# One unit less to spare, loads sized by the lead, a merged cache layout and the inverse root on GpSimd in a two-layer decode kernel

## Chip, cores, metric

One core of a Trainium2 chip. The metric is the device time of one launch in microseconds, as the median of several executions. The kernel before takes 2435.75 us (2431.96 to 2438.01, 12 runs).

## The reference

Two identical layers of attention over a cache, each followed by a small MLP, for one new token in each of 8 sequences. The same caches serve both layers, and the second layer's queries depend on the first layer's result.

```python
B, Sq, D = 8, 1, 640;  Hq, Hkv, Sk, Dh = 32, 32, 4096, 128;  Dff = 1728      # bf16
q = (layernorm(x) @ wq) per head;  p = softmax(q k^T / sqrt(Dh));  o = p v   # k, v: B x 32 x 4096 x 128
x = x + (o @ wo);   x = x + relu(layernorm(x) @ w1) @ w2
# ... and both lines once more, with the same k, v and weights
```

One cache is 8 x 32 x 4096 x 128 x 2 bytes = 268 MB. K and V, read in both layers, are 1074 MB. That is what the kernel is about.

## The kernel before

The work is cut into *visits*: a layer, a sequence `b` and a pair of heads `hp` (16 pairs). A visit reads a K tile and a V tile of 2 MB each. A tile has four *units* of 0.5 MB (128 partitions x 4 KB). SBUF holds an arena of 26 units. A planner in Python writes one static list of loads and engine work. Some units, loaded for layer 0, are kept until layer 1 of the same sequence, so they are not loaded twice. Between the two layers of `b`, the first four head pairs of sequence `b+1` have to pass through whatever units are left (`SPARE`), which take turns: a small ring; meanwhile the MLP of `b` and the queries of its layer 1 are worked off in small steps between the units.

```python
UNIT = 4; GP = 4; G = 26; SPARE = 6; SMALL = 4; AHEAD = 4; CAP = 20
...
    keep = set()                                   # the last pairs of heads; order1 visits them first
    for hp in order1:                              # order1 = 15, 14, 13, 0, 1, ...
        for which in "VK":
            for g in range(UNIT - 1, -1, -1):
                if len(keep) < G - SPARE:
                    keep.add((which, hp, g))
...
    def feed():                                    # called after every release of a unit
            ...
            roomy = G - len(kept)
            n = 4 if keeping or roomy >= 16 else 2 if roomy >= SMALL else 1
            while n > 1 and (g % n or any(...)):   # aligned, within the tile, same keeping
                n //= 2
            u = room(n)                            # n free units in a row, aligned to n
            if u is None:
                return
...
    def do_load(which, i, g, n, u):                # 16 KiB from one partition's row to the next
        src = (A_k_cache if which == "K" else A_v_cache)[b, hp]
        nc.sync.dma_start(out=arena[:, u * GW : (u + n) * GW], in_=src[:, g * GW : (g + n) * GW])
...
    def inverse_root(out, s2):                     # 1/sqrt for a layer norm of one sequence, all on VectorE
        ...                                        # four small instructions
        for n in range(4):                         # Newton steps
            nc.vector.scalar_tensor_tensor(out=v[:, 1:2], in0=y, scalar=v[:, 0:1], in1=y, op0=ALU.mult, op1=ALU.mult)
            nc.vector.scalar_tensor_tensor(out=dst, in0=v[:, 1:2], scalar=1.5, in1=y, op0=ALU.add, op1=ALU.mult)
```

## Time and profile before

| what | before | where it is read |
|---|---|---|
| time, median | 2435.75 us | 12 runs |
| bytes on the load queue | 1004.9 MB | DMA queues of the page |
| rate over the span / undisturbed / in a dip | 415 / 429 to 430 / about 361 GB/s | page, stretches |
| DMA in the chain that ended last | 82% | chain of waits |
| last load landed, span ended | 2416.1, 2432.6 us | completion counts in the trace |

The lines below are from the page of the kernel before: the DMA rows of the span in 40 equal slices (busy tenths, then GB/s), the load queue (packets, megabytes, share of 16 engines' span), the chain that ended last, and the issues by source (count, KB each, median us from issue to landing).

```profile
DMA  9999999999999999999999999999999999999997
GB/s 408 429 430 383 429 429 430 428 373 430 430 429 429 374 428 430 430 427 370 429 430 429 417 389 429 430 429 404 396 429 430 430 394 404 430 429 417 395 429 298
...
q1 hardware_dynamic: 83332, 1004.90, 98.6%
...
DMA 82%; PE 15%; DVE 2%; issue 1%; ACT 1%; SPq 0%; ACTq 0%
...
arena<-in_A_v_cache_dram SPq DMA_DIRECT2D x192, 2048.0 KB, 26.9
arena<-in_A_k_cache_dram SPq DMA_DIRECT2D x184, 2048.0 KB, 27.3
arena<-in_A_k_cache_dram SPq DMA_DIRECT2D x112, 1024.0 KB, 9.7
arena<-in_A_v_cache_dram SPq DMA_DIRECT2D x80, 1024.0 KB, 7.4
```

The engines are "busy" throughout, but the GB/s row shows the dips: one per sequence, eight in all. Two views say what is different in a dip. First, two stretches, an undisturbed one and most of a dip (busy time of each engine, clock, DMA share, GB/s); then what PE waited for in that dip (us in total, times, longest).

```profile
core 0: us, PE busy (x) PEld busy (x) DVE busy (x) ACT busy (x) POOL busy (x), PEclk, DMA share, GB/s
300.00:480.00 180.00, 81.81 (x1665) 47.79 (x1664) 23.14 (x117) 21.99 (x72) 0.00 (x0) 1.00 1.01 429
500.00:550.00 50.00, 39.14 (x854) 27.72 (x847) 13.30 (x75) 9.71 (x42) 0.00 (x0) 1.00 0.96 361
...
PE o_ps L458 <- DMA arena<-in_A_v_cache_dram: 10.3, 5, 4.8
PE s_ps L470 <- DMA arena<-in_A_k_cache_dram: 2.2, 4, 1.0
PE blk_ps L489 <- DVE diag L486: 1.8, 1, 1.8
```

In the undisturbed stretch PE works 82 of 180 us and only follows the loads. In the dip it still waits for loads, while the load queue waits for units to come free: the DMA share stays at 0.96, yet the rate falls to 361. The packets show it: those of the 1 MB loads took 334 ns on average at a median of 309, and a packet that is held up counts as busy. The rate is what to read. The third wait is VectorE's: a small reduction of the softmax stood behind the inverse root. The timeline of VectorE and PE (start, duration, line, instruction) shows it:

```profile
506.92 0.16 DVE L348 TENSOR_SCALAR root<-ch_ps 128x1 f32<-128x1 f32 x1 [0.61 <-PE ch_ps L330]
...
509.15 0.16 DVE L358 SCALAR_TENSOR_TENSOR rstd<-root 128x1 f32<-128x1 f32 x1
509.35 0.17 DVE L340 TENSOR_TENSOR xf<-xc,rstd 128x5 bf16<-128x5 f32 x1
509.43 0.27 DVE L484 TENSOR_REDUCE hmx<-blk_ps 2x1 f32<-2x128 f32 x1
509.73 0.15 DVE L486 TENSOR_TENSOR diag<-ident,hmx 2x2 bf16<-2x2 bf16 x1
509.94 0.16 PE L489 MATMUL blk_ps<-diag,onesb_c 2*128 2x2 bf16 x1 [1.82 <-DVE diag L486]
```

### The profile page before, as it was taken

The numbers are of one execution on the slowest core, as the hardware profiler recorded it, in microseconds if no ns is written. First come the engines' busy times: TensorE is split into PE (matmuls) and PEld (weight loads), VectorE is DVE, ScalarE is ACT, GpSimd is POOL, SyncE is SP. The second block draws the span as 40 slices with busy tenths as digits, with TensorE's granted clock in tenths as the row PEclk, the third lists the DMA queues.
The fourth block names the chain that finished last, engine by engine and source line by source line (L and its number), as shares of the span: only waits on it lengthen the run. The fifth ranks groups of instructions, "written<-read, shape, count | busy, mean of one in ns | idle before, by whom it ended". The sixth has DMA issues, their size and how long they took to land.

```text
span 2432.6 us, 57320 instructions
## 1 busy us (share of the span) xinstructions
PE 1272.9 (52%) x26486; PEld 788.4 (32%) x26486; DVE 380.7 (16%) x1984; ACT 337.4 (14%) x1179; POOL 0.7 (0%) x6
## 2 busy tenths in 40 slices
PE   3436644465444754447444574445744457445745
PEld 2224322343222422225222352223422234223523
DVE  1102111121111211112111121111211112111211
ACT  1101111111111111111111111111111111111111
POOL 0000000000000000000000000000000000000000
DMA  9999999999999999999999999999999999999997
GB/s 408 429 430 383 429 429 430 428 373 430 430 429 429 374 428 430 430 427 370 429 430 429 417 389 429 430 429 404 396 429 430 430 394 404 430 429 417 395 429 298
DMA packets 83572, 1008.57 MB, mean 415 GB/s; under 512 B 9348, under 2 KB 9348, under 8 KB 9348
## 3 DMA queue, kind: packets, MB, share of 16 engines
q1 hardware_dynamic: 83332, 1004.90, 98.6%
q8 instruction: 207, 3.39, 0.5%
q14 instruction: 33, 0.27, 0.0%
HBM read 1004.86 MB, written 0.01 MB: 413 GB/s over the span
## 4 chain that ended last, share of the span: by engine, by line
DMA 82%; PE 15%; DVE 2%; issue 1%; ACT 1%; SPq 0%; ACTq 0%
DMA arena<-in_A_k_cache_dram 42%; DMA arena<-in_A_v_cache_dram 38%; PE s_ps L470 5%; PE o_ps L458 5%; DMA w_sb<-in_B_w_dram 2%; PE q_ps L442 1%; DVE hmx L484 1%; DMA wo_sb<-in_A_wo_dram 1%; ACT o_sb L516 1%; PE oy_ps L521 1%; PE blk_ps L489 0%; DVE diag L486 0%; PE oy_ps L538 0%; PE blk_ps L480 0%; PE ch_ps L374 0%
## 5 line engine op out<-in xcount | busy, mean ns | idle before, releaser
L458 PE MATMUL o_ps<-arena,P_sb 128*4 128x512 bf16 x4096 | 556.9, 606 | 579.2 <-DMA arena<-in_A_v_cache_dram 575.8
L470 PE MATMUL s_ps<-q,arena 128*128 128x1 bf16 x16384 | 534.8, 165 | 510.4 <-DMA arena<-in_A_k_cache_dram 505.2
L470 PEld LDWEIGHTS <-arena 128*128 128x128 bf16 x16384 | 495.4, 104 | 539.1 <-DMA arena<-in_A_k_cache_dram 532.5
L458 PEld LDWEIGHTS <-P_sb 128*4 128x4 bf16 x4096 | 105.0, 83 | 681.8 <-issue 673.6
L493 ACT ACTIVATE nmax<-blk_ps 128x2 f32<-128x2 f32 x256 | 44.0, 172 | 1803.8 <-PE blk_ps L489 1803.8
L484 DVE TENSOR_REDUCE hmx<-blk_ps 2x1 f32<-2x128 f32 x256 | 71.3, 279 | 686.9 <-PE blk_ps L480 686.9
L516 ACT CAST o_sb<-o_ps 100x512 bf16<-100x512 f32 x256 | 149.8, 585 | 105.8 <-PE o_ps L458 105.8
L508 DVE TENSOR_REDUCE lsum<-blk_ps 128x2 f32<-128x64 f32 x256 | 57.5, 225 | 402.3 <-PE blk_ps L502 402.3
L497 ACT ACTIVATE P_sb<-s_ps,nmax 128x32 bf16<-128x32 f32 x512 | 119.0, 283 | 8.2
L476 DVE TENSOR_REDUCE mrow<-s_ps 128x2 bf16<-128x64 f32 x256 | 57.4, 224 | 252.9 <-PE s_ps L470 252.9
L502 PEld LDWEIGHTS <-onesb_c 128*128 128x128 bf16 x256 | 26.5, 104 | 203.6 <-issue 203.6
L480 PE MATMUL blk_ps<-ident,mrow 128*2 128x128 bf16 x256 | 79.5, 310 | 3.4 <-DVE mrow L476 3.4
L489 PEld LDWEIGHTS <-onesb_c 2*128 2x128 bf16 x256 | 25.2, 99 | 135.9 <-issue 135.9
L521 PE MATMUL oy_ps<-gsel,o_sb 100*128 100x2 bf16 x1024 | 63.8, 166 | 3.9 <-ACT o_sb L516 0.7
L531 DVE TENSOR_TENSOR oT<-oy_ps,invL 128x2 bf16<-128x2 f32 x128 | 20.4, 159 | 281.1 <-PE oy_ps L521 281.1
L531 DVE TENSOR_TENSOR o<-oy_ps,invL 128x2 bf16<-128x2 f32 x128 | 21.4, 167 | 274.7 <-PE oy_ps L521 274.7
L489 PE MATMUL blk_ps<-diag,onesb_c 2*128 2x2 bf16 x256 | 41.1, 160 | 42.7 <-DVE diag L486 14.4
L502 PE MATMUL blk_ps<-P_sb,onesb_c 128*128 128x64 bf16 x256 | 59.9, 234 | 1.1 <-ACT P_sb L497 1.1
L442 PE MATMUL q_ps<-xq,wq_sb 128*128 128x1 bf16 x1280 | 53.7, 166 | 4.2 <-issue 2.6
L538 PE MATMUL oy_ps<-oT,wo_sb 128*128 128x1 bf16 x1280 | 51.8, 165 | 0.0
L538 PEld LDWEIGHTS <-wo_sb 128*128 128x128 bf16 x1440 | 50.9, 105 | 0.8 <-issue 0.8
L442 PEld LDWEIGHTS <-wq_sb 128*128 128x128 bf16 x1280 | 44.9, 105 | 17.5 <-issue 16.7
(58 smaller groups left out, 408.3 us busy)
## 6 DMA issues: line engine op xcount, KB each, us to landing
arena<-in_A_v_cache_dram SPq DMA_DIRECT2D x192, 2048.0 KB, 26.9
arena<-in_A_k_cache_dram SPq DMA_DIRECT2D x184, 2048.0 KB, 27.3
arena<-in_A_k_cache_dram SPq DMA_DIRECT2D x112, 1024.0 KB, 9.7
arena<-in_A_v_cache_dram SPq DMA_DIRECT2D x80, 1024.0 KB, 7.4
wq_sb<-in_A_wq_dram SPq DMA_DIRECT2D x4, 1280.0 KB, 25.2
wo_sb<-in_A_wo_dram SPq DMA_DIRECT2D x4, 1280.0 KB, 35.8
w_sb<-in_B_w_dram SPq DMA_DIRECT2D x1, 2240.0 KB, 37.4
w_sb<-in_B_w_dram SPq DMA_DIRECT2D x1, 2160.0 KB
```

What stands on the lines that cost most here:

```text
L442: nc.tensor.matmul(q_ps[:, h : h + 1], lhsT=wq_sb[:, g, c, (2 * n + h) * Dh : (2 * n + h + 1) * Dh], rhs=xlns[b][:, 0, c : c + 1], start=( ...
L458: nc.tensor.matmul(o_ps[32 * c : 32 * c + CJ, :], lhsT=P_tiles[i][:, h, j : j + CJ], rhs=arena[:, at + c * CJ * Dh : at + (c + 1) * CJ * D ...
L470: nc.tensor.matmul(s_tiles[i][:, j : j + 1], lhsT=arena[:, at + n * P : at + (n + 1) * P], rhs=q, start=True, stop=True)
L480: nc.tensor.matmul(blk[i][:2, :P], lhsT=m_tiles.pop(i), rhs=ident, start=True, stop=True)
L484: nc.vector.tensor_reduce(out=hmx, in_=blk[i][:2, :P], axis=AX.X, op=ALU.max)
L489: nc.tensor.matmul(blk[i][:, P : P + 2], lhsT=ones_b, rhs=nmax.pop(i), start=True, stop=True)
L497: nc.scalar.activation(out=P_tiles[i][:, h, :], in_=S[:, h, :], func=ACT.Exp, bias=nm[:, h : h + 1], scale=inv_sqrt_dh)
L502: nc.tensor.matmul(blk[i][:, P + 2 :], lhsT=ones_p, rhs=P_tiles[i].rearrange("p h j -> p (h j)"), start=True, stop=True)
L508: nc.vector.tensor_reduce(out=L, in_=blk.pop(i)[:, P + 2 :].rearrange("p (h j) -> p h j", h=2), axis=AX.X, op=ALU.add)
L516: nc.scalar.copy(out=o_tiles[i][:OR], in_=o_ps[:OR, :].rearrange("p (j d) -> p j d", j=CJ))
L521: nc.tensor.matmul(oy[i][:, :2], lhsT=o_tiles[i][:OR, j, :], rhs=gsel[:OR, j, :], start=(j == 0), stop=(j == CJ - 1))
L538: nc.tensor.matmul(oy[i][:, 2 + c * nb : 2 + (c + 1) * nb], lhsT=wo_sb[:, 2 * hp + h, c * P : (c + 1) * P], rhs=o1[:, 2 * hp + h, :] if la ...
```

## The change

Its intent is to read fewer bytes and to keep the loads flowing. (1) One more unit is kept (`SPARE = 5`). (2) The size of a load follows the *lead*, the number of occupied units that are not kept: up to 8 units with a large lead, single units when the lead is small; kept units follow the same rule, where before they always came four at a time. (3) K and V go into one array in the order in which they are used, so that a load can run over tiles. (4) The last loads taper. (5) The inverse root moves to GpSimd, with three Newton steps instead of four and one more empty step before its result is used.

```diff
-SPARE = 6
-SMALL = 4
+SPARE = 5
+LEADS = ((12, 8), (8, 4), (7, 2))
+PASSING = ((16, 8), (13, 4), (11, 2))
+def tile_at(NP, which, hp):
+    return max(0, 2 * hp - 1) if which == "K" else min(2 * hp + 2, 2 * NP - 1)
...
     def room(n):
-        us = [u for u in range(0, G - n + 1, n) if not any(owner[u : u + n])]
+        us = [u for u in range(G - n + 1) if not any(owner[u : u + n])]
...
-            roomy = G - len(kept)
-            n = 4 if keeping or roomy >= 16 else 2 if roomy >= SMALL else 1
+            lead = sum(owner) - len(kept)
+            leads = PASSING if kept else LEADS
+            most = next((n for least, n in leads if lead >= least), 1)
+            most = min(most, max(1, (len(stream) - at[0]) // 2))
+            b, p, keeping = place(stream[at[0]])
+            n = 1
+            while n < most and place(stream[at[0] + n]) == (b, p + n, keeping):
+                n += 1
...
-        norm = [(0, "sums"), (2, "mean"), (0, "center"), (2, "var"), (0, "scale"), (1, None)]
+        norm = [(0, "sums"), (2, "mean"), (0, "center"), (2, "var"), (0, "scale"), (1, None), (1, None)]
...
-        nc.sync.dma_start(out=arena[:, u * GW : (u + n) * GW], in_=src[:, g * GW : (g + n) * GW])
+        nc.sync.dma_start(out=arena[:, u * GW : (u + n) * GW], in_=A_kv[b, :, p * GW : (p + n) * GW])
...
-        for n in range(4):
-            nc.vector.scalar_tensor_tensor(...)          # two per step, on VectorE
+        for n in range(3):
+            nc.gpsimd.tensor_tensor(out=t, in0=y, in1=y, op=ALU.mult)
+            nc.gpsimd.tensor_scalar(out=t, in0=t, scalar1=v[:, 0:1], scalar2=1.5, op0=ALU.mult, op1=ALU.add)
+            nc.gpsimd.tensor_tensor(out=dst, in0=t, in1=y, op=ALU.mult)
...
+    kv = np.empty((B, p, 2 * NP, 2 * Sk), A_k_cache.dtype)   # a partition's 32 tiles: 512 KiB
```

A side effect: neighbouring partitions' rows were 16 KiB apart in HBM, and a tile was one contiguous piece; now they are 512 KiB apart.

More of the change, by code (lines that the diff above doesn't have):

```diff
@@ L60, in plan @@
         layer, b, hp = visits[i]
-        gs = [g for g in range(UNIT) if layer == 0 or (which, hp, g) not in keep]
-        stream.append((which, i, gs))
+        stream += [(which, i, g) for g in range(UNIT) if layer == 0 or (which, hp, g) not in keep]
     weights = {}
@@ L70, in plan @@
     weights.setdefault(max(1, NP - 4), []).append(("w2",))
-    owner = [None] * G
+    owner = [False] * G
     freed = list(range(-G, 0))
@@ L75, in plan, with place @@
     ops, chains = [], []
-    at = [0, 0, 0]
+    at = [0, 0]
     def keeps(which, i, g):
         return visits[i][0] == 0 and (which, visits[i][2], g) in keep
+    def place(x):
+        return visits[x[1]][1], tile_at(NP, x[0], visits[x[1]][2]) * UNIT + x[2], keeps(*x)
     def room(n):
-        us = [u for u in range(0, G - n + 1, n) if not any(owner[u : u + n])]
+        us = [u for u in range(G - n + 1) if not any(owner[u : u + n])]
         return min(us, key=lambda u: max(freed[u : u + n])) if us else None
@@ L88, in feed @@
         while at[0] < len(stream):
-            which, i, gs = stream[at[0]]
-            if at[1] == len(gs):
-                at[:2] = at[0] + 1, 0
-                continue
-            if at[1] == 0 and which == "K":
-                ops.extend(("weights",) + w for w in weights.pop(i, []))
-            g = gs[at[1]]
-            keeping = keeps(which, i, g)
-            roomy = G - len(kept)
-            n = 4 if keeping or roomy >= 16 else 2 if roomy >= SMALL else 1
-            while n > 1 and (g % n or any(x not in gs or keeps(which, i, x) != keeping for x in range(g, g + n))):
-                n //= 2
+            lead = sum(owner) - len(kept)
[6 more added lines that the diff above has]
+                n += 1
             u = room(n)
@@ L103, in feed @@
                 return
-            for k in range(n):
+            for k, (which, i, g) in enumerate(stream[at[0] : at[0] + n]):
+                ops.extend(("weights",) + w for w in weights.pop(i, []) if which == "K")
                 owner[u + k] = True
-                where[which, i, g + k] = u + k
+                where[which, i, g] = u + k
                 if keeping:
-                    kept[which, visits[i][1], visits[i][2], g + k] = u + k
-            ops.append(("load", which, i, g, n, u))
-            at[1] += n
+                    kept[which, b, visits[i][2], g] = u + k
+            ops.append(("load", b, p, n, u))
+            at[0] += n
     def find(which, i, g):
@@ L122, in release @@
             u = kept.pop(key)
-        at[2] += 1
-        owner[u], freed[u] = None, at[2]
+        at[1] += 1
+        owner[u], freed[u] = False, at[1]
         feed()
@@ L210 @@
     A_x: bass.AP,
-    A_k_cache: bass.AP,
-    A_v_cache: bass.AP,
+    A_kv: bass.AP,
     A_wq: bass.AP,
@@ L224 @@
     B, Sq, D = A_x.shape
-    _, NP, Dh, W = A_k_cache.shape
-    H = 2 * NP
+    H = A_wo.shape[1] // D
+    NP = H // 2
+    Dh = A_kv.shape[1]
+    W = A_kv.shape[2] // (2 * NP)
     Sk = W // 2
@@ L335, in scale @@
                 inverse_root(rstd, st[key, "var"])
+                nc.gpsimd.tensor_scalar(
+                    out=xln[:, 0, :], in0=st[key, "xc"][:, 0, :], scalar1=rstd, scalar2=None, op0=ALU.mult
+                )
             else:
@@ L339, in scale @@
                 nc.vector.reciprocal(out=rstd, in_=std)
-            nc.vector.tensor_tensor(out=xln, in0=st[key, "xc"], in1=_free(rstd, [(1, nb), (0, DC)]), op=ALU.mult)
+                nc.vector.tensor_tensor(out=xln, in0=st[key, "xc"], in1=_free(rstd, [(1, nb), (0, DC)]), op=ALU.mult)
         return dict(sums=sums, mean=mean, center=center, var=var, scale=scale)
@@ L348, in inverse_root @@
         nc.vector.tensor_scalar(out=v[:, 0:1], in0=s2, scalar1=1.0 / D, scalar2=eps, op0=ALU.mult, op1=ALU.add)
-        nc.vector.tensor_scalar(out=i[:, 1:2], in0=i[:, 0:1], scalar1=1, scalar2=None, op0=ALU.logical_shift_right)
-        nc.vector.tensor_scalar(
-            out=i[:, 2:3], in0=i[:, 1:2], scalar1=-1.0, scalar2=1597463007.0, op0=ALU.mult, op1=ALU.add
+        nc.gpsimd.tensor_scalar(
+            out=i[:, 2:3], in0=i[:, 0:1], scalar1=-0.5, scalar2=1597463007.0, op0=ALU.mult, op1=ALU.add
         )
-        nc.vector.tensor_scalar(out=v[:, 0:1], in0=v[:, 0:1], scalar1=-0.5, scalar2=None, op0=ALU.mult)
+        nc.gpsimd.tensor_scalar(out=v[:, 0:1], in0=v[:, 0:1], scalar1=-0.5, scalar2=None, op0=ALU.mult)
         y = v[:, 2:3]
-        for n in range(4):
-            nc.vector.scalar_tensor_tensor(out=v[:, 1:2], in0=y, scalar=v[:, 0:1], in1=y, op0=ALU.mult, op1=ALU.mult)
-            dst = out if n == 3 else v[:, 3:4] if n % 2 == 0 else v[:, 2:3]
-            nc.vector.scalar_tensor_tensor(out=dst, in0=v[:, 1:2], scalar=1.5, in1=y, op0=ALU.add, op1=ALU.mult)
+        t = v[:, 1:2]
+        for n in range(3):
+            nc.gpsimd.tensor_tensor(out=t, in0=y, in1=y, op=ALU.mult)
+            nc.gpsimd.tensor_scalar(out=t, in0=t, scalar1=v[:, 0:1], scalar2=1.5, op0=ALU.mult, op1=ALU.add)
+            dst = out if n == 2 else v[:, 3:4] if n == 0 else v[:, 2:3]
+            nc.gpsimd.tensor_tensor(out=dst, in0=t, in1=y, op=ALU.mult)
             y = dst
@@ L419, in do_finish, with do_load @@
             steps[2] = steps[2] or op == "add"
-    def do_load(which, i, g, n, u):
-        layer, b, hp = visits[i]
-        src = (A_k_cache if which == "K" else A_v_cache)[b, hp]
-        nc.sync.dma_start(out=arena[:, u * GW : (u + n) * GW], in_=src[:, g * GW : (g + n) * GW])
+    def do_load(b, p, n, u):
+        nc.sync.dma_start(out=arena[:, u * GW : (u + n) * GW], in_=A_kv[b, :, p * GW : (p + n) * GW])
     def do_q0(g):
@@ L550 @@
                 L=do_l, I=do_i, OC=do_oc, OG=do_og, O=do_o, W=do_w, Y=do_y, C=do_finish, Q0=do_q0, Q=do_q, QC=take_q)
-    with tc.manual_schedule(engines={ENG.PE, ENG.DVE, ENG.Activation, ENG.SP}):
+    with tc.manual_schedule(engines={ENG.PE, ENG.DVE, ENG.Activation, ENG.Pool, ENG.SP}):
         xT_ps = ps.tile([P, B * DC], FP32, name="ch_ps")
@@ L577, in _laid_out @@
     w2[:Dff] = B_w2
+    k = A_k_cache.reshape(B, NP, 2, Sk, Dh).transpose(0, 1, 4, 2, 3).reshape(B, NP, Dh, 2 * Sk)
+    v = A_v_cache.reshape(B, NP, 2, UNIT, NJ // UNIT, p, Dh).transpose(0, 1, 5, 3, 2, 4, 6).reshape(B, NP, p, -1)
+    kv = np.empty((B, p, 2 * NP, 2 * Sk), A_k_cache.dtype)
+    for hp in range(NP):
+        kv[:, :, tile_at(NP, "K", hp)] = k[:, hp]
+        kv[:, :, tile_at(NP, "V", hp)] = v[:, hp]
+    kv = kv.reshape(B, p, -1)
     return {
         "A_x": c(A_x),
-        "A_k_cache": c(A_k_cache.reshape(B, NP, 2, Sk, Dh).transpose(0, 1, 4, 2, 3)).reshape(B, NP, Dh, 2 * Sk),
-        "A_v_cache": c(A_v_cache.reshape(B, NP, 2, UNIT, NJ // UNIT, p, Dh).transpose(0, 1, 5, 3, 2, 4, 6)).reshape(
-            B, NP, p, 2 * NJ * Dh
-        ),
+        "A_kv": kv,
         "A_wq": c(A_wq.reshape(DC, p, NG, HD // NG).transpose(1, 2, 0, 3)).reshape(p, -1),
```

## The prediction

> **What bounds it.** Part 2 of the page has the DMA engines at 9 tenths or more in every slice but the last, mean 415 GB/s; the chain of waits is 82% DMA. PE is busy 52%. Part 3 counts 1004.9 MB on the load queue. In undisturbed stretches the stretch table shows 429 to 431 GB/s with 2 MB loads. At that rate the bytes need about 2337 us of the 2433. The other 95 us are about 14 us at the ends (the last load lands at about 2416) and eight dips, one per batch, of about 50 us each at about 355 GB/s (slices of 370 to 390), some 8 us lost in each. A dip is where 20 units of 0.5 MB are kept for the second layer and the next batch's first four head pairs pass through 6 spare units as 1 MB loads. There PE waits for arena loads (10.3 us for V alone in 500 to 545 us), and the queue for PE: latency of a small ring.
>
> **What the change does, on the critical path.**
> 1. SPARE 5 keeps one more unit per batch: 8 x 0.524 MB = 4.2 MB fewer, about -10 us.
> 2. Passing with 5 single units instead of 3 pairs. The shortest time from issue to landing is 5.2 us for a pair, so about 2.7 us fixed plus 2.5 transfer. A pair's cycle is 5.2 + about 2.1 on PE + 0.2 = 7.5 us against 7.4 us of transfer for three: no slack. A single's is about 2.7 + 1.2 + 1.0 + 0.2 = 5.1 us against 6.1: one us of slack. An issue costs the queue only 0.33 us. The ceiling falls: 8 KB rows take 309 ns, 16 KB rows 611 ns, so about 6 ns per row, and 4 KB rows would reach about 416 GB/s. I expect about 395 in the dips: -30 us over eight dips (at best -50), and +6 us for more single loads around them.
> 3. Loads of up to 8 units (32 KB rows) outside the dips: 430 to 432 GB/s, about -8 us.
> 4. Tapered last loads: one unit instead of four for PE after the last landing, -2 us.
> 5. Inverse root on GpSimd: frees some 2.6 us of DVE twice a batch; an added empty step covers its latency. Near zero outside item 2.
>
> The sum is -44 us: 2392.
>
> **The cost I can't size.** The merged layout makes consecutive partitions' rows 512 KiB apart in HBM (before: 16 KiB, whole tiles contiguous). The Trainium skill, "DMA: Bandwidth & Descriptors", section "Latency and other measured facts", has copies at a 512 KiB row pitch at 207 GB/s against 214 in full, 3% less. No trace here shows it. That would be +70 us; I give it less than even odds and add a few us.
>
> **Prediction: 2398 us, 2366 to 2450 in 8 of 10.** Chances: faster by over 2% 0.32, within 2% 0.62, slower by over 2% 0.06.
>
> **What would show it.** Load bytes 1000.7 MB. Steady stretches at 430 to 432 GB/s: item 3 right and no pitch loss; at 415 to 425: pitch loss, with 16 engines still fully busy and packets slower per byte. Dips at 385 to 410 instead of 355: item 2 right. PE's waits for xf near zero: item 5 right. Last landing to end a few us shorter: item 4.
>
> **What would make it wrong.** A pitch loss of over 2%; GpSimd stalling PE before the up-projection; single loads draining the buffer; or dips staying at 355.

## The result

| | before | after |
|---|---|---|
| time, median | 2435.75 us | 2391.67 us (2389.81 to 2395.99, 8 runs) |
| ratio | | 0.9822 (95%: 0.9812 to 0.9831) |
| bytes on the load queue | 1004.9 MB | 1000.7 MB |
| mean of the page's slices at 425 GB/s or more | 429.3 | 431.2 GB/s |
| dips: microseconds lost against 430 GB/s, eight together | 62.6 | 36.2 us |
| last load landed to end of span | 16.5 | 14.4 us |

Ratios here are the mean time of one kernel's fast runs over that of the other's of the same rounds, so not quite the ratio of the medians quoted. The row on dips is worked out from the trace's DMA packets: the rate in each microsecond, and 1 - rate/430 summed over the stretches around the eight passings where the rate, smoothed over 8 us, is below 424. It is one profiled execution per kernel, so a few us of it are chance.

The page of the kernel after, the lines that answer to those of before:

```profile
DMA  9999999999999999999999999999999999999997
GB/s 410 431 429 405 429 431 433 426 402 432 429 434 423 394 433 429 433 423 401 432 432 431 416 411 434 430 432 406 413 430 431 432 407 424 430 432 415 411 433 308
...
q1 hardware_dynamic: 99028, 1000.72, 99.3%
...
DMA 78%; PE 17%; DVE 1%; issue 1%; ACT 1%; POOL 1%; SPq 0%; ACTq 0%; DVEq 0%
...
arena<-in_A_kv_dram SPq DMA_DIRECT2D x129, 4096.0 KB, 24.7
arena<-in_A_kv_dram SPq DMA_DIRECT2D x423, 512.0 KB, 6.5
arena<-in_A_kv_dram SPq DMA_DIRECT2D x78, 2048.0 KB, 22.4
```

The dips of the GB/s row went from between 370 and 396 (lowest slice of each) to between 394 and 411, and the slices between them from 429 to 431. The same dip as before, and PE's waits in it. By the definition above it now runs from about 477 to 546 us of the span, before from 497 to 553, so the stretch shown lies 5 us earlier:

```profile
core 0: us, PE busy (x) PEld busy (x) DVE busy (x) ACT busy (x) POOL busy (x), PEclk, DMA share, GB/s
495.00:545.00 50.00, 40.82 (x876) 29.04 (x879) 9.84 (x52) 9.28 (x41) 5.31 (x24) 1.00 1.00 402
...
PE o_ps L467 <- DMA arena<-in_A_kv_dram: 3.5, 8, 0.6
PE s_ps L479 <- DMA arena<-in_A_kv_dram: 3.1, 9, 0.5
PE ch_ps L385 <- POOL xf L343: 0.7, 1, 0.7
```

PE's waits for V in the dip fell from 10.3 us to 3.5, the longest from 4.8 us to 0.6. The wait for `diag` is gone and one of 0.7 us for GpSimd has come. The timeline shows what GpSimd's chain takes, from the first instruction on VectorE to the normalized `xf`:

```profile
500.34 0.16 DVE L358 TENSOR_SCALAR root<-ch_ps 128x1 f32<-128x1 f32 x1 [0.35 <-PE ch_ps L337]
...
503.83 0.32 POOL L343 TENSOR_SCALAR xf<-xc,rstd 128x5 bf16<-128x5 f32 x1
504.20 0.54 PE L385 MATMUL ch_ps<-xf,w_sb 128*128 128x1 bf16 x15 [0.71 <-POOL xf L343]
```

That is 3.8 us (500.34 to 504.15) with three Newton steps, where VectorE took 2.6 us (506.92 to 509.52) with four.

So the total came out near where the prediction put it (2398 us). Whether its parts did, the experiments had to say.

### The profile page after: what moved, and what is told of

The parts are those of the page before. It is cut to its first block, busy times and chain, and to the rows that moved or that the text cites. A ratio compares the mean times of both kernels' runs of the same rounds, so it can differ in the third digit from the quotient of the medians.

```text
span 2388.9 us, 57534 instructions
## 1 busy us (share of the span) xinstructions
PE 1288.4 (54%) x26486; PEld 795.6 (33%) x26486; DVE 351.1 (15%) x1792; ACT 338.8 (14%) x1179; POOL 43.2 (2%) x198
## 4 chain that ended last, share of the span: by engine, by line
DMA 78%; PE 17%; DVE 1%; issue 1%; ACT 1%; POOL 1%; SPq 0%; ACTq 0%; DVEq 0%
DMA arena<-in_A_kv_dram 77%; PE s_ps L479 6%; PE o_ps L467 6%; PE q_ps L451 2%; ACT o_sb L525 1%; DVE hmx L493 1%; PE oy_ps L530 1%; DMA wo_sb<-in_A_wo_dram 1%; PE blk_ps L498 0%; PE oy_ps L547 0%; DVE diag L495 0%; PE blk_ps L489 0%; POOL root L367 0%; PE ch_ps L337 0%; POOL root L366 0%
## 5 line engine op out<-in xcount | busy, mean ns | idle before, releaser
L479 PE MATMUL s_ps<-q,arena 128*128 128x1 bf16 x16384 | 542.3, 166 | 622.4 <-DMA arena<-in_A_kv_dram 615.7
L467 PE MATMUL o_ps<-arena,P_sb 128*4 128x512 bf16 x4096 | 562.7, 604 | 415.8 <-DMA arena<-in_A_kv_dram 413.1
L498 PE MATMUL blk_ps<-diag,onesb_c 2*128 2x2 bf16 x256 | 41.7, 163 | 25.1
L530 PEld LDWEIGHTS <-o_sb 100*128 100x128 bf16 x1024 | 47.3, 106 | 22.7 <-ACT o_sb L525 21.9
```

The source lines that it names most:

```text
L467: nc.tensor.matmul(o_ps[32 * c : 32 * c + CJ, :], lhsT=P_tiles[i][:, h, j : j + CJ], rhs=arena[:, at + c * CJ * Dh : at + (c + 1) * CJ * D ...
L479: nc.tensor.matmul(s_tiles[i][:, j : j + 1], lhsT=arena[:, at + n * P : at + (n + 1) * P], rhs=q, start=True, stop=True)
L498: nc.tensor.matmul(blk[i][:, P : P + 2], lhsT=ones_b, rhs=nmax.pop(i), start=True, stop=True)
L530: nc.tensor.matmul(oy[i][:, :2], lhsT=o_tiles[i][:OR, j, :], rhs=gsel[:OR, j, :], start=(j == 0), stop=(j == CJ - 1))
```

## The experiments

The prediction's theory: fewer bytes, and a ring of single units that has slack (time to spare before PE must wait for the next unit) where three pairs had none. Rivals: the inverse root on VectorE makes the dips; or the large loads carry the gain. Each kernel below gave a correct result and was timed in five rounds against the kernel before on the same chip. "Dip loss" is the sum over the eight dips defined above, from the run's profile.

| run | what it is | median us | ratio to before (95%) | dip loss us |
|---|---|---|---|---|
| e1 | before + 5 spare units, singles | 2425.85 | 0.9963 (0.9949 to 0.9976) | 64.9 |
| e2 | before + 5 spare units, pairs | 2490.95 | 1.0231 (1.0211 to 1.0250) | 128.9 |
| e3 | before + root on GpSimd | 2439.71 | 1.0021 (1.0008 to 1.0033) | 64.2 |
| e4 | after, root on VectorE | 2399.50 | 0.9855 (0.9841 to 0.9868) | 46.1 |
| e5 | after, kept units four at a time | 2396.09 | 0.9842 (0.9830 to 0.9855) | 37.1 |
| e6 | e1 + singles for kept units, and from 15 kept on | 2418.71 | 0.9933 (0.9919 to 0.9946) | 50.9 |
| e7 | after, loads of at most 4 units | 2401.03 | 0.9860 (0.9847 to 0.9873) | 41.7 |
| e8 | after, 4 MiB between rows | 4379.47 | 1.7994 (1.7952 to 1.8037) | - |
| e9 | after, 6 spare units | 2394.94 | 0.9834 (0.9821 to 0.9846) | 30.2 |
| e10 | after, no taper | 2396.90 | 0.9840 (0.9827 to 0.9853) | 40.1 |
| e11 | e6 + root on GpSimd | 2418.16 | 0.9928 (0.9914 to 0.9941) | 55.2 |
| e12 | e11 in the merged layout | 2406.29 | 0.9875 (0.9853 to 0.9896) | 43.1 |
| after | the change | 2391.67 | 0.9822 (0.9812 to 0.9831) | 36.2 |

### e1: the two constants alone

```diff
-SPARE = 6
-SMALL = 4
+SPARE = 5
+SMALL = 6
```

By this constant single loads start only when all 21 units are kept; with fewer kept, the loads that are not kept are still pairs, and kept units still come four at a time.

> The kernel before with two constants changed: 5 spare units, loaded one at a time while units are kept; old layout, old loads of 4 elsewhere, inverse root on VectorE. Theory (fewer bytes and a ring with slack explain most of the gain): 2402 us, range 2396 to 2408, that is -10 us of bytes and about -24 us in the dips, whose mean rises from about 373 to about 400 GB/s. Rival R (the dips come from the inverse root that holds VectorE): only the bytes, about 2426 us, dips still near 373. Rival L (the large loads matter most): about 2426 or slower.

Measured: 2425.85 us. The bytes were saved (1000.7 MB) and the dips did not become any shallower: 64.9 us lost against 62.6. The stretch of the same dip in this run:

```profile
500.00:550.00 50.00, 40.22 (x848) 28.07 (x848) 13.30 (x75) 9.74 (x42) 0.00 (x0) 1.00 0.96 365
```

This is just the number of the rival that lets only the bytes count, and the theory as stated fell. The next two runs ask what single units are worth, and whether the root is the cause.

### e2: five units, but pairs

```diff
-SPARE = 6
+SPARE = 5
```

> The kernel before with 5 spare units but still pairs while units are kept, so two pairs and at times a left-over single. Theory (ring without slack): the dips deepen below 373 GB/s and eat the 10 us of saved bytes or more: 2430 to 2460 us. Rival R and any theory in which only bytes count: 2426 us.

Measured: 2490.95 us, 2.3% slower than before and 31 us above the range expected, with a dip loss of 128.9 us, twice that of before. The stretch of the same dip:

```profile
500.00:550.00 50.00, 28.89 (x617) 20.83 (x618) 10.95 (x63) 5.89 (x24) 0.00 (x0) 1.00 0.83 297
```

Here even the share of the DMA engines falls, to 0.83. So five spare units in pairs do starve: they cost 65 us more as pairs than as singles. Single units are what make it possible to give up the sixth, but they are not what made the dips shallower.

### e3 and e4: the inverse root, moved alone and put back alone

e3 is the kernel before with the root, the scaling and the step list of the change; e4 is the change with those of before.

```diff
-        nc.vector.scalar_tensor_tensor(...)      # e3: these become the nc.gpsimd lines of the change
+        nc.gpsimd.tensor_tensor(...)             # e4: the other way round
-        norm = [..., (0, "scale"), (1, None)]
+        norm = [..., (0, "scale"), (1, None), (1, None)]
```

> The kernel before with only the inverse root and the scaling moved to GpSimd and the added empty step. Theory: 2430 us, range 2424 to 2437; VectorE's reductions wait less, but the small ring stays. Rival R: about 2410 us, with dips near 400 GB/s.

> The changed kernel with the inverse root, the scaling and the step list of before put back. Theory: 2393 to 2400 us, at most a few us slower than the change. Rival R: about 2415 us, dips back towards 373 GB/s.

Measured: alone it costs about 5 us (0.2%, the interval excludes 1; 2439.71 us is also above the range expected), and putting the old root back into the change costs 7.8 us, with a dip loss of 46.1 us instead of 36.2. The rival with the root as the main cause falls on both. But the move is not worth nothing either, as the prediction had it outside the dips. In e4 VectorE's waits are back, in the list of PE's waits over the whole span:

```profile
PE blk_ps L494 <- DVE diag L491: 8.4, 8, 1.1
PE blk_ps L485 <- DVE mrow L481: 5.2, 6, 1.0
```

That is 13.6 us, where the change has two waits for GpSimd instead, for the normalized inputs of the MLP (`xf`) and of the next queries (`xq`):

```profile
PE ch_ps L385 <- POOL xf L343: 4.6, 7, 0.8
PE q_ps L451 <- POOL xq L343: 3.2, 7, 0.7
```

The difference of 5.8 us is near the 7.8 us measured, but it does not explain them. e6 and e11 below differ in the same waits by as much, 8.2 + 4.2 us in e6:

```profile
PE blk_ps L489 <- DVE diag L486: 8.2, 8, 1.1
PE blk_ps L480 <- DVE mrow L476: 4.2, 6, 0.9
```

and 4.1 + 2.6 us in e11:

```profile
PE ch_ps L378 <- POOL xf L336: 4.1, 7, 0.7
PE q_ps L446 <- POOL xq L336: 2.6, 5, 0.6
```

Yet e11 is no faster than e6. The worth of the move in the change is timed; its cause is not shown.

### e5 and e6: kept units a tile at a time

Laying the units side by side, each with its issue, its landing and PE's first matmul on it, showed another difference. In e1 the last kept tile is one load of four units in front of the units that pass. PE then gets four units at once that free nothing. The timeline of PE in e1 at the entry of a dip: the four V units of the kept tile, then the passing units one by one.

```profile
500.39 0.60 PE L458 MATMUL o_ps<-arena,P_sb 128*4 128x512 bf16 x4 [3.85 <-DMA arena<-in_A_v_cache_dram]
...
506.66 0.60 PE L458 MATMUL o_ps<-arena,P_sb 128*4 128x512 bf16 x4
...
508.38 0.60 PE L458 MATMUL o_ps<-arena,P_sb 128*4 128x512 bf16 x4 [1.02 <-DMA arena<-in_A_v_cache_dram]
...
510.93 0.60 PE L458 MATMUL o_ps<-arena,P_sb 128*4 128x512 bf16 x4 [0.49 <-DMA arena<-in_A_v_cache_dram]
```

A wait of 3.85 us for the block, then passing units 1.7 and 2.6 us apart instead of 1.2 (part of the 2.6 is a wait of 0.8 us for VectorE's `diag`). I took this for the cause and tested it both ways.

```diff
 # e5, in the change
+            if keeping:
+                most = UNIT - stream[at[0]][2]
 # e6, in e1
-            n = 4 if keeping or roomy >= 16 else 2 if roomy >= SMALL else 1
+            n = 4 if roomy >= 16 else 2 if roomy >= SMALL else 1        # SMALL = 12
```

> The changed kernel, but the units that are kept are loaded a tile (4 units) at a time again, as before the change, not by the lead. Theory K (the block in front of the passing units is what starves the ring: its four units land at one moment, PE then works on units whose release frees nothing, and the first freed place comes several us late): 2403 to 2414 us, 10 to 20 us slower than the change, with the loss in the dips at 47 to 58 us instead of 36. Rival (only the loads of the passing units and the layout count): within 3 us of the change.

> The kernel before with 5 spare units, single loads while 15 or more units are kept, and this rule for the kept units too (they were exempt in the run with five single units); old layout, old loads of 4 elsewhere, inverse root on VectorE. Theory K: 2400 to 2412 us, dips losing about 45 us in all. Rival (the merged layout, the lead rule or the large loads are needed): about 2426 us as without it.

Measured: e5 loses 4.4 us by the medians, at intervals that barely overlap, and its profile shows no deeper dips (37.1 us; the profile is of its fastest run). e6 gains 7 us over e1, with intervals apart and a dip loss of 50.9 us (again the fastest run, 5 us below the median). But e6 changes two things: with `SMALL = 12` single loads also start at 15 kept units instead of 21, and its trace has 32 loads of 1 MB where e1 has 72. So the block is at most part of it, at less than half the size I expected. e6 still stood 19 us behind e4, although both have singles, kept singles and the root on VectorE.

### e7: no loads above four units

```diff
-LEADS = ((12, 8), (8, 4), (7, 2))
-PASSING = ((16, 8), (13, 4), (11, 2))
+LEADS = ((8, 4), (7, 2))
+PASSING = ((13, 4), (11, 2))
```

> The changed kernel with loads of at most 4 units (16 KB rows) instead of 8. Theory (rows of 32 KB are worth 0.5% of the steady stretches): 2396 to 2402 us. Rival (large loads carry the gain): 2410 us or more.

Measured: 9.4 us slower than the change. Its page's slices at 425 GB/s or more average 429.3, as before the change, not 431.2. By the packets of the traces a 32 KB row takes 1213 ns, a 16 KB row 611, an 8 KB row 309 and a 4 KB row 159: about 8 ns of each are independent of the length (159 - (309 - 159) = 9; 611 - 2 x (611 - 309) = 7). Large loads are worth 9 us, as predicted (8). The run's dip loss is also larger (41.7 us instead of 36.2), so part of the 9 us may lie in the dips, within what chance does to that figure.

### e8: 4 MiB between rows

The prediction had a cost that it could not size: the pitch. At 512 KiB no loss was visible. Was the figure of the Trainium skill ("DMA: Bandwidth & Descriptors", section "Latency and other measured facts": copies at a row pitch of 4 MiB run at 103 GB/s instead of 214) of any use for a stream of reads?

```diff
-in_=A_kv[b, :, p * GW : (p + n) * GW]
+in_=A_kv[:, b, p * GW : (p + n) * GW]       # and the host lays it out (p, b, tile)
```

> The changed kernel with the cache laid out partition first, so that the rows of neighbouring partitions lie 4 MiB apart in HBM instead of 512 KiB. If the loss that the Trainium skill gives for copies at such pitches also holds for a stream of reads into SBUF (about half the rate), 4000 us or more. If reads of 16 to 32 KB per row from one core don't feel it: 2392 us. I lean to a loss of some per cent: 2450 us.

Measured: 4379.47 us. The rate row of its page:

```profile
GB/s 261 359 184 140 214 294 311 176 140 258 309 284 164 143 265 293 278 151 136 259 292 284 153 146 265 301 283 151 152 278 315 249 149 167 281 287 192 134 244 228
DMA packets 99270, 1004.40 MB, mean 229 GB/s; under 512 B 11092, under 2 KB 11092, under 8 KB 65236
```

The page's factor of about one half holds here for reads into SBUF: 229 GB/s on average against 420, with the same loads. Short rows suffer more than long ones: a 4 KB packet took 364 ns on average instead of 163, an 8 KB packet 830 instead of 311, a 32 KB packet 1687 instead of 1216. I had leaned to a few per cent, and was wrong. At 512 KiB, where the skill's copies lost 3% (207 of 214), this kernel lost nothing that shows: the measurement decides.

### e9 and e10: ring size and taper

```diff
 # e9
-SPARE = 5
+SPARE = 6
 # e10
-            most = min(most, max(1, (len(stream) - at[0]) // 2))
+            most = min(most, len(stream) - at[0])
```

> The changed kernel with 6 spare units, as before the change, and everything else new: 4.2 MB more bytes (+9.8 us), a ring of six single units. If the ring of 5 is what still limits the dips of the change, their loss falls from 36 to about 20 us and the time is 2383 to 2390 us, better than both kernels. If the dips are at the ceiling of 4 KB rows plus stalls on PE, their loss stays above 28 us: 2393 to 2402 us.

> The changed kernel without the taper of the last loads (the last one is then 4 units, and 8 before it). Theory: 2393 to 2397 us, 2 to 5 us slower than the change, all of it after the last load was issued. Rival (no effect): 2391.7 us.

Measured: with six units the dips lose 30.2 us instead of 36.2, which the 4.2 MB more of bytes eat up: 2394.94 us, not better than the change (the intervals overlap). By the expectation this is the second case (2393 to 2402 us, a loss above 28 us, though 30.2 lies near that border): the ring of five is not what mostly limits the dips of the change. The traces fit that. Take the single loads that are not kept, issued while all kept units are held. In the change such a load takes 5.8 us (median of 203) from issue to the landing on its last engine, with six spare units 7.0 us (median of 177); but one load lands 1.23 us after the other (median) in both. So the time to landing includes a wait behind other loads, and it grows with the ring. It can't be held against the 5.1 us of the prediction's cycle to say whether the "one us of slack" is there; that stays open. What the estimate did leave out is that the 16 engines finish such a load about 2 us apart (3.3 us with six units).

Without the taper the last load landed 16.8 us before the end instead of 14.4. The taper is worth 2.4 us there; the medians differ by 5.2 us at overlapping intervals.

### e11 and e12: the layout alone

e7 and e6 pass through a dip with nearly the same list of load sizes, but e7 has the root on GpSimd and the merged layout. e11 gives e6 the root, e12 gives e11 the layout, by the very same list of loads.

```diff
 # e12, against e11
-        src = (A_k_cache if which == "K" else A_v_cache)[b, hp]
-        nc.sync.dma_start(out=arena[:, u * GW : (u + n) * GW], in_=src[:, g * GW : (g + n) * GW])
+        p = tile_at(NP, which, hp) * UNIT + g
+        nc.sync.dma_start(out=arena[:, u * GW : (u + n) * GW], in_=A_kv[b, :, p * GW : (p + n) * GW])
```

> The kernel of the run with five single units and single loads for the kept ones too, plus the inverse root on GpSimd and the added empty step. Theory I (the root pays only once the ring keeps up, because a stall of PE then empties it): 2408 to 2413 us, 6 to 10 us less than without the root. Rival (in the old plan the root costs 4 us, as alone): 2420 us or more.

> The kernel of the run with five single units, single loads for the kept ones and the root on GpSimd, with one thing changed: it reads the merged layout of the change (rows of neighbouring partitions 512 KiB apart) by the very same list of loads. Theory H (4 KB rows land sooner or more evenly at this pitch than as quarters of a contiguous tile at 16 KiB pitch): 2400 to 2407 us, ratio to before 0.985 to 0.988, dips losing about 42 us in all. Rival (the layout is neutral, the gap to the change with loads of 4 lies in its lead rule and its taper): about 2418 us, ratio 0.993. If the 512 KiB pitch costs as the Trainium skill's copies did, over 2440 us.

Measured: e11 at 2418.16 us is no better than e6, against the theory tested. e12 at 2406.29 us is 12 us better by the layout alone (the two ran on different chips, so the ratios to the kernel before count: 0.9875 against 0.9928, intervals apart). One dip and one undisturbed stretch, e11:

```profile
500.00:550.00 50.00, 38.53 (x801) 26.91 (x801) 8.59 (x46) 8.83 (x40) 5.27 (x24) 1.00 0.98 378
300.00:480.00 180.00, 82.00 (x1684) 48.41 (x1682) 23.38 (x118) 21.99 (x72) 0.00 (x0) 1.00 1.01 430
```

and e12, the same stretches:

```profile
500.00:550.00 50.00, 41.83 (x895) 29.08 (x895) 9.72 (x51) 9.83 (x42) 5.30 (x24) 1.00 1.02 405
300.00:480.00 180.00, 81.82 (x1661) 47.81 (x1657) 23.50 (x119) 22.73 (x74) 0.00 (x0) 1.00 1.01 429
```

The layout does nothing for 2 MB loads (429 or 430 GB/s in both) and lifts the dip of single loads from 378 to 405 GB/s; over all eight dips the loss falls from 55.2 to 43.1 us, which is the 12 us. The packets agree: the time that 4 KB packets took beyond their usual 159 ns adds up to 26.8 us per engine in e11 and 18.7 in e12. Why quarters of a contiguous tile are held up more often than rows 512 KiB apart is not shown by any run.

## Why the prediction was right

By the ratios, times 2435.8 us, the steps from before to after are: five units and singles -9 (e1), singles for the kept units and from 15 kept on -7 (e6), the root -1 (e11), the layout -13 (e12), the lead rule with taper and free placement -4 (e7), loads of eight -9. The sum is -43; predicted were -44 before the allowance for the pitch. Each of these differences has an uncertainty of 3 to 6 us (95%, from the intervals), and their order matters: e4 puts the root at -8.

- *What bounds it* was right. Everything that helped, helped by bytes or by the rate of the loads.
- *Item 1*, 4.2 MB less, -10 us: right. The bytes are as stated and e1 gained 9 us.
- *Item 2*, passing with single units, -30 + 6 us in the dips: the size was right and the reason was not. The dips did lose 26 us less (predicted 24) and run near 400 GB/s, so the check that the prediction named for this item (385 to 410) was met without its reason. But single units in place of pairs only kept the dips from doubling with a unit less (e1 against e2); by themselves they gained nothing (e1: 64.9 us lost, before 62.6). As far as the runs show, the gain came from three things the item did not name: the merged layout, 12 us (e12 against e11); the kept units no longer loaded as blocks, at most 7 us in the old plan (e6, with its earlier singles) and about 4 in the new one (e5, within the noise); and the root on GpSimd, about 8 us in the full change (e4). These are timed differences from different bases, so they need not add up exactly. The step that failed is "Passing with 5 single units instead of 3 pairs" as the source of the -30 us: alone it left the loss at 64.9 us. Whether the sum under it, "one us of slack", is wrong in itself stays open (e9).
- *Item 3*, loads of up to 8 units, -8 us: right. e7 puts it at 9 us, and the slices rose from 429.3 to 431.2.
- *Item 4*, taper, -2 us: right, 2.4 us from e10's last landing to its end.
- *Item 5*, the root near zero outside item 2: right alone (e3: +5, e11: nothing), and worth 8 us in the full change, for a reason that is not shown. PE's waits for `xf` were small but not near zero, 4.6 us in all. Theory I, that it pays as soon as the ring keeps up, fell with e11, which has the ring but not the layout. What it needs besides is open.
- *The cost it couldn't size*, the pitch: it had the wrong sign. The allowance of 6 us was unneeded; the layout is the largest single step.

The lesson of the total is modest. The prediction was 2398 us, 6 us above the result; its sum before the allowance, 2392, met the 2391.67 us by luck, because one large term was right by compensation. Only the experiment that did that part alone (e1) showed it. None of the variants beat the change.

## What to carry to other kernels

When a change bundles several ideas, run the one that your sum leans on most by itself: a total that fits does not confirm its terms. In a stream bound by loads, look at the rate and not at the busy share of the DMA engines, and do not judge a small ring by the time from issue to landing under load, which grows with the ring (5.8 us with five units, 7.0 with six, at the same pace of landings): a run with one unit more tells more (e9). A layout is part of a load's cost: in this kernel, with the same list of loads, 512 KiB between rows was 12 us better than contiguous tiles for 4 KB rows, and 4 MiB between rows made the kernel 1.8 times as long.

## What the Trainium skill lacked or had wrong

- "DMA: Bandwidth & Descriptors", section "Latency and other measured facts": it gives a loss of 3% for copies at a row pitch of 512 KiB. Reads into SBUF lost nothing here with 16 KB rows, the length of the page's copies (429 GB/s against 430 from contiguous tiles, e12 against e11), nor visibly with 32 KB rows (slices at 431 GB/s), and with 4 KB rows they ran better than from contiguous tiles (405 against 378 GB/s in a dip, e12 against e11). At 4 MiB the page's factor of one half held (229 GB/s against 420).
- The same page, section "Measured (HBM→SBUF, 128 partitions, SWDGE, issued from GpSimd)": its rule to batch to 1 MiB or more for 75% of peak leaves out that loads in flight overlap. With at most five loads of 0.5 MB in flight from SP, a dip of the change ran at 396 GB/s (496 to 529 us), 92% of the undisturbed 431.
- "DMA: Bandwidth & Descriptors", section "Why a DMA increments its semaphore by 16 and not by 1", says that the engines of a load finish independently; none of the pages read says how far apart under load. It was 2.1 us for a 0.5 MB load in a passing (median of 203 loads, first to last completion count, kernel after), more than the 1.2 us its data take, and 3.3 us with one more unit in the ring (177 loads, e9).
- "GPSIMD Engine Reference", section "Engine selection": elementwise work with two inputs belongs on VectorE because GpSimd is slower. It is slower here (3.8 us for the root's chain with three Newton steps against 2.6 with four), and still the move was worth 8 us in the full change (e4), though alone it cost 5 us (e3); no page tells these cases apart, and neither do the runs.
